# Moving the preparation of MLP 2's weight pairs to other steps of MLP 1

## The chip, the cores and the metric

The kernel runs on one core of one Trainium2 chip. The metric is device time in microseconds (us). Three runs of the kernel before took 1110.99, 1112.35 and 1111.3 us, so the median is 1111.3 us. A separate profiled execution of it took 1110.82 us, and its span from the first to the last instruction is 1109.0 us.

## The reference

Windowed attention with eight memory keys over 3072 tokens of width 512 is followed by two MLPs with a hidden width of 2048. Weights come as 64-bit floats and are rounded to 32 bits on the chip.

```python
def _moe_ref(x, w_in, w_out):       # MLP 1
    h = x @ w_in
    g = h - np.tanh(h)
    return (g @ w_out).astype(np.float32)

def _moe2_ref(x, w_in, w_out):      # MLP 2
    h = x @ w_in
    g = np.where(h >= 1, h, np.where(h <= -1, 0.0, (h + 1) ** 2 / 4))
    return (g @ w_out).astype(np.float32)

x = attention(q, k, v, mem_k, mem_v)     # chunks of 32, left 16, right 8
x = _moe_ref(x, **moe); return _moe2_ref(x, **moe2)
```

## The kernel before, in words

The engines are named as in the profile: PE multiplies matrices, DVE is the vector engine, ACT the activation engine, SP issues the transfers (DMAs). PSUM is the memory that PE writes to. Every engine works through a list of instructions in the order in which the program was written, and an instruction that waits holds up all that stand behind it on its engine.

Every operand of a product is kept as a high and a low half (`hi`, a rounded copy made on ACT; `lo`, the rest, subtracted on DVE by `split_to`, lines 224 and 225), and a product is the sum of three: hi x hi, hi x lo, lo x hi.

**MLP 1** works on six blocks of 512 tokens. Each block takes 16 steps, one for every 128 hidden columns, so there are 96 steps, 0 to 95. A step has `hidden` (12 matmuls into a PSUM tile `h`, of which there are two), and `gate` (tanh on ACT, a subtraction on DVE that frees `h` for the step after the next). On DVE each step also makes the low half of the weights two steps ahead (`split_weights_lo`, tile `wlo0`). In steps 16 to 79 a step also has `output`, the second product of the step 16 earlier (blocks 0 to 3, again 12 matmuls), whose weights SP loads again for each block (`w1o_load`, line 196). Attention for the later blocks runs between the steps up to step 78, one group of 128 tokens every four steps (`slot_v`, `slot_s`, `slot_exp`, `slot_b`).

The second product of the last two blocks is made after step 95 with fewer multiplications, from sums of quarters (Strassen and Winograd): seven passes of eight products, `G(-1, 0)` to `G(-1, 55)`, each of six matmuls (`last_product`, line 815). The quarters of MLP 1's second weights that these need are the "own" sums: `own_raw`, `prep_sums` and `own_split`, placed by `OWN_AT`. The sums of the gated values are `g_sums` (lines 683 to 686), and each pass product needs a split of its values on ACT and DVE (`prepare`, tiles `ghi` and `glo`, five of each).

**MLP 2** does both its products in that way, on three stretches of 1024 tokens (`sb` = 0, 1, 2): products `P(sb, q, i)` with q = 0 to 7 and i from 1 to 7 (`product`, line 727), then passes `G(sb, k)`. After a product 1 or 6, ACT copies the PSUM tile out (`take_copy`, line 651, tiles `u1`, `u2`), after a 5 the same into `v`; only then may PE go on in that tile, with product 6, 7 or 3. Products 2, 7, 3 and 4 each end in a gate (`gate2`: an addition on DVE, line 661, two ACT instructions, lines 665 and 666, and one on DVE, line 669).

MLP 2's weights are prepared in 16 **pairs** (`PAIRS`; eight of the first weights, eight of the second). Preparing one pair takes
- `prep_load`: two DMAs of 512 KB;
- `prep_act`: four ACT instructions (lines 136 and 139);
- `prep_rest`, twice: four DVE instructions each (lines 145, 146, 154, 159);
- `prep_sums`: four DVE instructions on half tiles (line 220);
- `prep_split`, four parts: a high half on ACT (224), a low half on DVE (225);
- `prep_store`: seven DMAs of 256 KB.

The dictionaries `before`, `rounds` and `behind` say what is written at which step: `before` and `rounds` ahead of `hidden` and `gate` of the next step, `behind` after them. `late` holds what is written among the products that follow the steps; its second part counts only products 1, 4, 2 and 7 of sb = 0 ("events").

```python
        run(before, i)
        run(rounds, i)
        hidden(i + 1, EARLY_N if i + 1 < 2 else 0)
        gate(i + 1)
        run(behind, i)
        if 0 <= o < PLAIN:
            output(o)
```

Eleven pairs begin in MLP 1 at steps 33, 37, 41, ..., 77 (every 4.4 steps); two are prepared among the passes G(-1), at k = 6 to 38; the last three among the products of sb = 0, one item at every event.

Of the kernel before, what the change touches and what calls it, by code (L numbers as in the profile page):

```python
# [30 lines left out]
KC = DM // 128  # L31
FC = DFF // 128
# [24 lines left out]
HALF = FC // 2  # L57
NSB = NB // 2
PAIRS = [(w, q) for w in range(2) for q in range(HALF)]
PREP, PREP_EVERY, PREP_FIRST, PREP_LATE = 33, 4.4, 11, 2  # L60
STREAM = 10
W1O, GSETS = 4, 5
EXTRA = 0

PLAIN = (NB - 2) * FC
OWN_AT = {q: 2 * FC + (0 if q % 2 == 0 else FC) + 2 * q for q in range(HALF)}

SPACE_A = (3, 4)

# [7 lines left out]
def tile_memory_attention_two_mlps(  # L77
# [463 lines left out]
    spare = []  # L541
# [62 lines left out]
    NG2 = len(PASSES) * HALF  # L604
# [193 lines left out]
    def last_product(e):  # L798
        _, sb, k = e
        i, q = PASSES[k // HALF], k % HALF  # L800
        a = i in (1, 6, 7, 4)
        if q == 0 and i in (1, 2, 5):
            bank[a] = [ps_g[0].tile([128, 512], F32, tag=f"g{c}{1 - a}", name=f"acc{i}_{sb}_{c}") for c in range(2)]
        rests()
        prepare(sb, k)
        hi_g, lo_g = gsplit.pop((sb, k))
        tag, t = w_t.pop(e)
        hi, lo = t[:, :256], t[:, 256:]
        first, last = i in (1, 2, 5) and q == 0, q == HALF - 1
        products = [(j, c) for j in range(3) for c in range(2)]  # L810
        if last:
            products.sort(key=lambda p: p[1])
        for j, c in products:
            w, g = ((hi, hi_g), (lo, hi_g), (hi, lo_g))[j]
            nc.tensor.matmul(  # L815
                bank[a][c], w[:, c * 128:(c + 1) * 128], g,
                start=first and j == 0, stop=last and j == 2, skip_group_check=True,
            )
        load_w(tag)
        flush()  # L820
        if k in SUMS_AT[sb < 0]:
            g_sums(sb, *SUMS_AT[sb < 0][k])
        for j in range(1, GSETS):
            prepare(sb, k + j)
        if last:
            done(sb, i, bank[a])
        nxt = sb + 1
        if nxt < NSB:
            for f, *args in x_at[sb < 0].get(k, ()):
                f(nxt, *args)  # L830

    x_at = [
        {2: [(x_load,)], 8: [(x_sum, 5)], 10: [(x_sum, 6)], 12: [(x_sum, 7)], 14: [(x_sum, 3)]},
        {18: [(x_load,)], 22: [(x_sum, 5)], 24: [(x_sum, 6)], 26: [(x_sum, 7)], 28: [(x_sum, 3)]},
    ]
    for n, i in enumerate((1, 2, 6, 5, 7, 3, 4)):
        for k in range(2):
# [33 lines left out]
            else:  # L871
                nc.sync.dma_start(out=out[(dm + c) * 128:(dm + c + 1) * 128, b * N:(b + 1) * N], in_=y[c])

    late = [{}, {}]
    for n, p in enumerate(PAIRS[PREP_FIRST:]):
        f = [
            (prep_act, *p), (prep_rest, *p, 0), (prep_rest, *p, 1), (prep_sums, *p),
            (prep_split, *p, 0), (prep_split, *p, 1), (prep_split, *p, 2), (prep_split, *p, 3),
        ]
        f = [[x] for x in f] + [[] for _ in range(1)]  # L880
        for m in range(4):
            f[5 + m].insert(0, (prep_store, *p, m))
        if n + PREP_FIRST + 1 < len(PAIRS):
            f[3].append((prep_load, *PAIRS[n + PREP_FIRST + 1]))
        for k, x in enumerate(f):
            if n < PREP_LATE:
                late[0].setdefault(6 + 2 * (8 * n + k), []).extend(x)
            else:
                late[1].setdefault(8 * (n - PREP_LATE) + k, []).extend(x)

    before, rounds, behind = {}, {}, {}

    def at_step(events, i, f, *args):
        assert i >= 0
        events.setdefault(int(i), []).append((i, f, args))


    for t in range(PER, NG + 1):
        k = t - PER
        i = SPACE_A[0] * min(k, PER) + SPACE_A[1] * max(0, k - PER)  # L900
# [12 lines left out]
    for w in range(2):  # L913
        for fc in range(FC):
            p = fc - EARLY + w * (FC + 2)
            assert p < fc + w * LAG - 2 + w
            if p >= 0:
# [3 lines left out]
                at_step(rounds, p, round_rest, 0, w, fc)  # L921
    for q, o in OWN_AT.items():
        at_step(rounds, o, own_raw, q, o - FC)
# [3 lines left out]
        at_step(before, o + 2, prep_store, 2, q, 1)  # L927
        at_step(before, o + 3, prep_store, 2, q, 2)
    for n, pair in enumerate(PAIRS):
        p = int(PREP + PREP_EVERY * n)  # L930
        if n > PREP_FIRST:
            break
        at_step(behind, p - 3, prep_load, *pair)
        if n == PREP_FIRST:
            break
        at_step(before, p, prep_act, *pair)
        at_step(rounds, p, prep_rest, *pair, 0)
        at_step(rounds, p + 1, prep_rest, *pair, 1)
        at_step(behind, p + 1, prep_sums, *pair)
        for m in range(4):  # L940
            at_step((rounds, behind)[m % 2], p + 2 + m // 2, prep_split, *pair, m)
            at_step(before, p + 3 + m // 2 + 0.1 * m, prep_store, *pair, m)
# [4 lines left out]
    LAST = NS - FC  # L947
# [3 lines left out]
    for i in range(STREAM):  # L951
        at_step(before, LAST + 1 + i // 2, stream_in)
    for q in range(HALF // 2):
        at_step(behind, LAST + 2 * q + 1, g_sums, -1, q, 0)
        at_step(behind, LAST + 2 * q + 2, g_sums, -1, q, 1)
    for k in range(3):
        at_step(behind, NS - 4 + k, prepare, -1, k, True)
        if k < 2:
# [11 lines left out]
    for j in range(PER):  # L970
        w = 0, 0, j
        pool, tag = ((ps_a, "a"), (ps_acc, "acc0"))[j % 2]
        pair = pool.tile([128, 2, 512], F32, tag=tag, name=f"start_a{j}")
# [80 lines left out]
    events = 0  # L1054
    for e in plan:
        if e[0] == "P":
            product(e)
        else:
            last_product(e)
        f = []  # L1060
        if e[0] == "G" and e[1] < 0:
            f = late[0].pop(e[2], [])
            if e[2] == NG2 - 1:
                spare.extend(f"y{i}" for i in range(KC))
        elif e[0] == "P" and e[1] == 0 and e[3] in (1, 4, 2, 7):
            f = late[1].pop(events, [])
            events += 1
            if not late[1] and f:
                spare.extend(f"prep{i}" for i in range(9))
        for f, *args in f:  # L1070
            f(*args)
    assert not late[0] and not late[1]
    assert not before and not rounds and not behind


# [46 lines left out]
```

## Time and profile before

| | |
|---|---|
| median of three runs | 1111.3 us |
| profiled execution, its span | 1110.82 us, 1109.0 us |
| PE busy | 1068.8 us (96%) |
| DVE busy | 858.0 us (77%) |
| ACT busy | 641.3 us (58%) |
| PE, DVE in the passes G(-1, 15) to G(-1, 33), 39.3 us | 31.6 us, 34.8 us |
| PE, DVE, ACT among products of sb = 0, 73.3 us | 59.0 us, 53.7 us, 48.5 us |

Busy time is the time in which at least one instruction runs on the engine. Matmuls overlap: the record of one is longer than the distance to the next, so a product's length is read from the starts. DVE instructions overlap slightly in the same way.

### The profile page before, as it was taken

What the parts mean: (1) busy time and instruction counts of PE and PEld (TensorE: products, weight loads), DVE (VectorE), ACT (ScalarE), POOL (GpSimd) and SP (SyncE); (2) the same over time, 40 slices, a digit from 0 to 9 for tenths busy, and PEclk for the clock granted to TensorE, in tenths of its full rate; (3) what the DMA queues carried; (4) which work ended last, traced back from release to release, by engine and by line L of the source; (5) the groups of instructions that cost most, each with busy time, mean ns of one, the idle gap of its engine ahead of it and who ended that gap; (6) DMA issues with size and microseconds to landing.
All of it is one profiled execution on the core that took longest, in us unless ns stands there. A gap on an engine that the chain in (4) does not pass through costs nothing.

```text
span 1109.0 us, 21044 instructions
## 1 busy us (share of the span) xinstructions
PE 1068.8 (96%) x7607; PEld 862.5 (78%) x7607; DVE 858.0 (77%) x1520; ACT 641.3 (58%) x1128; POOL 42.6 (4%) x38
## 2 busy tenths in 40 slices
PE   7899999999999999999989978899999999999998
PEld 3677888888888888888857855687888888888887
DVE  4799977799898987767889677688567697467854
ACT  3566665555555554544656566766467766477553
POOL 1132221000000000000000000000000000000000
PEclk8999999999999999999999999999999999999999
DMA  9997885899898999634479876786776787766674
GB/s 221 255 249 202 261 243 178 257 299 315 283 308 269 290 276 329 219 118 139 125 270 319 267 234 226 223 262 210 231 214 193 208 273 212 234 192 194 197 207 150
DMA packets 211944, 259.36 MB, mean 234 GB/s; under 512 B 65409, under 2 KB 128897, under 8 KB 211841
## 3 DMA queue, kind: packets, MB, share of 16 engines
q1 hardware_dynamic: 211840, 258.01, 76.2%
q8 instruction: 61, 1.00, 0.4%
q14 instruction: 43, 0.34, 0.1%
HBM read 199.23 MB, written 58.72 MB: 233 GB/s over the span
## 4 chain that ended last, share of the span: by engine, by line
PE 87%; DVE 5%; ACT 4%; DMA 2%; issue 1%; SPq 0%; DVEq 0%; ACTq 0%
PE h L488 24%; PE acc L815 20%; PE acc L526 16%; PE qa L727 9%; PE qc L727 4%; PE qb L727 2%; PE acc_-1_0_6986 L815 2%; PE acc_-1_1_6987 L815 2%; PE a L392 1%; PE a L336 1%; ACT t L665 1%; ACT t L666 1%; PE b L378 1%; DVE g L661 1%; PE start_tx L963 1%
## 5 line engine op out<-in xcount | busy, mean ns | idle before, releaser
L815 PE MATMUL acc<-ghi,inG 128*128 128x512 f32 x672 | 183.1, 389 | 0.0
L501 ACT ACTIVATE g<-h 128x512 f32<-128x512 f32 x96 | 57.4, 598 | 196.2 <-PE h L488 159.6
L727 PE MATMUL qa<-xc,inP 128*128 128x512 f32 x576 | 145.6, 399 | 13.8 <-ACT u L651 11.8
L815 PEld LDWEIGHTS acc<-ghi,inG 128*128 128x128 f32 x672 | 126.1, 188 | 26.2
L225 DVE TENSOR_TENSOR glo<-g,ghi 128x512 fp32r<-128x512 f32 x174 | 118.0, 687 | 31.7 <-ACT ghi L224 30.9
L727 PEld LDWEIGHTS qa<-xc,inP 128*128 128x128 f32 x576 | 109.1, 191 | 42.6 <-ACT u L651 15.6
L224 ACT ACTIVATE ghi<-g 128x512 fp32r<-128x512 f32 x174 | 107.5, 627 | 46.5 <-PE acc L815 23.0
L815 PE MATMUL acc<-glo,inG 128*128 128x512 f32 x336 | 107.2, 390 | 0.4 <-DVE glo L225 0.3
L502 DVE TENSOR_TENSOR g<-h,g 128x512 f32<-128x512 f32 x96 | 66.1, 688 | 53.4 <-ACT g L501 52.1
L488 PE MATMUL h<-xh,whi 128*128 128x512 f32 (+2 forms) x392 | 105.4, 391 | 0.0
L488 PE MATMUL h<-xl,whi 128*128 128x512 f32 (+2 forms) x392 | 104.0, 387 | 0.1
L488 PE MATMUL h<-xh,wlo 128*128 128x512 f32 (+2 forms) x392 | 103.7, 386 | 0.0
L665 ACT ACTIVATE t<-g,half 128x512 f32<-128x512 f32 x72 | 52.2, 724 | 74.5 <-DVE g L661 74.5
L488 PEld LDWEIGHTS h<-xl,whi 128*128 128x128 f32 x392 | 73.0, 188 | 15.4 <-DVE xl L423 0.2
L488 PEld LDWEIGHTS h<-xh,wlo 128*128 128x128 f32 x392 | 73.0, 188 | 14.8
L178 DVE TENSOR_TENSOR wlo<-raw,whi 128x512 fp32r<-128x512 f32 x112 | 79.6, 711 | 5.1 <-ACT whi L171 5.1
L488 PEld LDWEIGHTS h<-xh,whi 128*128 128x128 f32 x392 | 71.8, 188 | 15.0 <-ACT xh L418 0.3
L171 ACT ACTIVATE whi<-raw 128x512 fp32r<-128x512 f32 x112 | 70.1, 626 | 8.0 <-POOL raw L159 8.0
L815 PEld LDWEIGHTS acc<-glo,inG 128*128 128x128 f32 x336 | 62.9, 188 | 14.7 <-DVE glo L225 1.9
L727 PE MATMUL qc<-xc,inP 128*128 128x512 f32 x288 | 73.5, 391 | 0.5 <-ACT v L651 0.5
L526 PE MATMUL acc<-ghi,whi 128*128 128x512 f32 x256 | 74.0, 403 | 0.0
L526 PE MATMUL acc<-ghi,wlo 128*128 128x512 f32 x256 | 70.7, 390 | 0.0
(713 smaller groups left out, 1802.5 us busy)
## 6 DMA issues: line engine op xcount, KB each, us to landing
inP<-part SPq DMA_DIRECT2D x168, 256.0 KB, 3.0
inG<-part SPq DMA_DIRECT2D x168, 256.0 KB, 2.9
stage<-w_in SPq DMA_DIRECT2D x32, 512.0 KB, 5.5
stage<-w_out SPq DMA_DIRECT2D x32, 512.0 KB, 4.7
part<-preph SPq DMA_DIRECT2D x64, 256.0 KB, 4.3
whi<-w1o SPq DMA_DIRECT2D x48, 256.0 KB, 4.9
wlo<-w1o SPq DMA_DIRECT2D x48, 256.0 KB, 5.0
part<-prepl SPq DMA_DIRECT2D x48, 256.0 KB, 4.5
```

Source lines behind the costliest of these rows:

```text
L171: nc.scalar.activation(out=hi, in_=r, func=AF.Copy)
L178: nc.vector.tensor_tensor(out=lo, in0=r, in1=hi.bitcast(F32), op=ALU.subtract)
L224: nc.scalar.activation(out=hi, in_=src, func=AF.Copy)
L225: nc.vector.tensor_tensor(out=lo, in0=src, in1=hi.bitcast(F32), op=ALU.subtract)
L336: nc.tensor.matmul(sp[j * CHUNK:(j + 1) * CHUNK, hh, pr, :], qt[j][hh * D:(hh + 1) * D, pr, :], kt[j][hh * D:(hh + 1) * D, pr, :], start=T ...
L488: nc.tensor.matmul(hp, w[:, kc * 128:(kc + 1) * 128], x[:, kc, n0:n1], start=j == 0 and kc == 0, stop=j == 2 and kc == KC - 1,)
L501: nc.scalar.activation(out=g, in_=hp, func=AF.Tanh)
L502: nc.vector.tensor_tensor(out=g, in0=hp, in1=g, op=ALU.subtract)
L526: nc.tensor.matmul(acc_t[dm], w[:, dm * 128:(dm + 1) * 128], g, start=first and j == 0, stop=last and j == 2,)
L665: nc.scalar.activation(out=t, in_=h, func=AF.Relu, scale=0.5, bias=half)
L727: nc.tensor.matmul(o, w[:, k * 128:(k + 1) * 128], z[k], start=i in (1, 2, 5) and j == 0 and k == 0, stop=j == 2 and k == 1, skip_group_ch ...
L815: nc.tensor.matmul(bank[a][c], w[:, c * 128:(c + 1) * 128], g, start=first and j == 0, stop=last and j == 2, skip_group_check=True,)
```

## The change

A pair now begins every four steps, at steps 30, 34, ..., 78, and two more at 83 and 90: fifteen pairs in MLP 1. None is prepared among the passes G(-1). The sixteenth, (1, 7), has one item at every third event, from event 2 to event 26 (the last only stores). The own sums go from steps 32, 36, 40, 44 and 50, 54, 58, 62 to 48, 52, 56, 60 and 66, 70, 74, 78 (in `OWN_AT` blocks are counted from the step; the second product of a step stands 16 steps behind it, so these are blocks 2 and 3 of the outputs). `g_sums` for q = 0 to 3 go two steps later. The load of the next stretch's input (`x_load`) goes from G(-1, 18) to G(-1, 14).

```diff
-PREP, PREP_EVERY, PREP_FIRST, PREP_LATE = 33, 4.4, 11, 2
+PREP_AT = [30 + 4 * n for n in range(13)] + [83, 90]
+PREP_FIRST = len(PREP_AT)
...
-OWN_AT = {q: 2 * FC + (0 if q % 2 == 0 else FC) + 2 * q for q in range(HALF)}
+OWN_AT = {q: 3 * FC + (0 if q % 2 == 0 else FC) + 2 * q for q in range(HALF)}
...
-        {18: [(x_load,)], 22: [(x_sum, 5)], ...
+        {14: [(x_load,)], 22: [(x_sum, 5)], ...
...
-    late = [{}, {}]
-    for n, p in enumerate(PAIRS[PREP_FIRST:]):
+    late = {}
+    for p in PAIRS[PREP_FIRST:]:
...
-            if n < PREP_LATE:
-                late[0].setdefault(6 + 2 * (8 * n + k), []).extend(x)
-            else:
-                late[1].setdefault(8 * (n - PREP_LATE) + k, []).extend(x)
+            late[2 + 3 * k] = x
...
-        at_step(behind, LAST + 2 * q + 1, g_sums, -1, q, 0)
-        at_step(behind, LAST + 2 * q + 2, g_sums, -1, q, 1)
+        at_step(behind, LAST + 2 * q + 3, g_sums, -1, q, 0)
+        at_step(behind, LAST + 2 * q + 4, g_sums, -1, q, 1)
...
-        if e[0] == "G" and e[1] < 0:
-            f = late[0].pop(e[2], [])
...
-            f = late[1].pop(events, [])
+            f = late.pop(events, [])
```

Three places show what this does to the lists. The first is DVE between the low weight halves of steps 86 and 87 (`wlo0_86`, `wlo0_87`), near the end of MLP 1; before, these were:

```order
L178 TENSOR_TENSOR wlo0_86_6734<-raw00_6_833,whi0_86_6732 128x512
L502 TENSOR_TENSOR g85_6753<-h85_6740,g85_6753 128x512
L686 TENSOR_TENSOR g82_6673<-g66_5645,g82_6673 128x512
L178 TENSOR_TENSOR wlo0_87_6759<-raw00_7_897,whi0_87_6757 128x512
L502 TENSOR_TENSOR g86_6778<-h86_6765,g86_6778 128x512
```

And now (line numbers are one higher; `raw11`, `stage11` and `sums1` belong to a pair):

```order
L179 TENSOR_TENSOR wlo0_86_6833<-raw00_6_833,whi0_86_6831 128x512
L146 TENSOR_SCALAR raw11_13_6801<-raw11_13_6801 128x512
L147 TENSOR_SCALAR raw11_13_6801<-raw11_13_6801 128x512
L155 SCALAR_TENSOR_TENSOR raw11_13_6801<-stage11_13_6728,raw11_13_6801 128x512
L160 ISA raw11_13_6801<-stage11_13_6728,raw11_13_6801 128x1024
L503 TENSOR_TENSOR g85_6856<-h85_6843,g85_6856 128x512
L221 TENSOR_TENSOR sums1_5_6859<-raw11_5_6798 128x256
L221 TENSOR_TENSOR sums1_5_6859<-raw11_13_6801,raw11_5_6798 128x256
L221 TENSOR_TENSOR sums1_5_6859<-raw11_13_6801,sums1_5_6859 128x256 x2
L687 TENSOR_TENSOR g80_6658<-g64_5422,g80_6658 128x512
L179 TENSOR_TENSOR wlo0_87_6867<-raw00_7_897,whi0_87_6865 128x512
```

A second `prep_rest` stands ahead of the gate of step 85, and `prep_sums` between that gate and the weights of step 87.

The second place is DVE in the passes, from the low half for G(-1, 26) on (`glo2`; `s5`, `s6`, `a7`, `a4` and `xc1` are the input sums of the next stretch). Before:

```order
L225 TENSOR_TENSOR glo2_-1_26_7367<-s1_-1_2_6781,ghi2_-1_26_7366 128x512
L590 TENSOR_TENSOR s5_0_0_7370<-a7_0_0_7298,a4_0_0_7300 128x512
L590 TENSOR_TENSOR s5_0_1_7371<-a7_0_1_7299,a4_0_1_7301 128x512
L225 TENSOR_TENSOR glo2_-1_27_7390<-s1_-1_3_6826,ghi2_-1_27_7389 128x512
L225 TENSOR_TENSOR glo2_-1_28_7408<-s1_-1_4_7013,ghi2_-1_28_7407 128x512
L590 TENSOR_TENSOR s6_0_0_7411<-s5_0_0_7370,xc1_0_7296 128x512
L590 TENSOR_TENSOR s6_0_1_7412<-s5_0_1_7371,xc1_0_7296 128x512
L145 TENSOR_SCALAR raw11_4_7375<-raw11_4_7375 128x512
L146 TENSOR_SCALAR raw11_4_7375<-raw11_4_7375 128x512
L154 SCALAR_TENSOR_TENSOR raw11_4_7375<-stage11_4_7195,raw11_4_7375 128x512
L159 ISA raw11_4_7375<-stage11_4_7195,raw11_4_7375 128x1024
L225 TENSOR_TENSOR glo2_-1_29_7428<-s1_-1_5_7054,ghi2_-1_29_7427 128x512
```

Now:

```order
L226 TENSOR_TENSOR glo2_-1_26_7509<-s1_-1_2_6962,ghi2_-1_26_7508 128x512
L591 TENSOR_TENSOR s5_0_0_7512<-a7_0_0_7392,a4_0_0_7394 128x512
L591 TENSOR_TENSOR s5_0_1_7513<-a7_0_1_7393,a4_0_1_7395 128x512
L226 TENSOR_TENSOR glo2_-1_27_7525<-s1_-1_3_7007,ghi2_-1_27_7524 128x512
L226 TENSOR_TENSOR glo2_-1_28_7543<-s1_-1_4_7201,ghi2_-1_28_7542 128x512
L591 TENSOR_TENSOR s6_0_0_7546<-s5_0_0_7512,xc1_0_7390 128x512
L591 TENSOR_TENSOR s6_0_1_7547<-s5_0_1_7513,xc1_0_7390 128x512
L226 TENSOR_TENSOR glo2_-1_29_7559<-s1_-1_5_7242,ghi2_-1_29_7558 128x512
```

The four instructions of `prep_rest` are gone from between the low halves; the input sums stay where they were.

The third place is ACT among the products of sb = 0, from the gate of product P(0, 1, 4) on (`t2_0_1_21`) to the copy of product 6 of q = 2 (`u2_0_2`). Before:

```order
L665 ACTIVATE t2_0_1_21_8111<-qa0_1_7953,half_83 128x512
L666 ACTIVATE t2_0_1_21_8111<-t2_0_1_21_8111 128x512
L136 ACTIVATE raw11_6_8115<-stage11_6_7969 128x512
L139 ACTIVATE stage11_6_7969<-stage11_6_7969 128x512
L136 ACTIVATE raw11_14_8118<-stage11_14_7971 128x512
L139 ACTIVATE stage11_14_7971<-stage11_14_7971 128x512
L651 ACTIVATE u2_0_2_8129<-qa0_2_8071 128x512
L665 ACTIVATE t2_0_2_11_8143<-g2_0_2_11_8141,half_83 128x512
```

Now:

```order
L666 ACTIVATE t2_0_1_21_8169<-qa0_1_8039,half_83 128x512
L667 ACTIVATE t2_0_1_21_8169<-t2_0_1_21_8169 128x512
L652 ACTIVATE u2_0_2_8184<-qa0_2_8134 128x512
L666 ACTIVATE t2_0_2_11_8198<-g2_0_2_11_8196,half_83 128x512
L667 ACTIVATE t2_0_2_11_8198<-t2_0_2_11_8198 128x512
```

The four instructions of `prep_act` no longer stand ahead of that copy; the remaining pair's four stand ahead of `u1_0_1`, at event 2.

## Rows read from the trace of the kernel before

**Rows 1.** The page: span, and busy time of the engines

```profile
span 1109.0 us, 21044 instructions
PE 1068.8 (96%) x7607; PEld 862.5 (78%) x7607; DVE 858.0 (77%) x1520; ACT 641.3 (58%) x1128; POOL 42.6 (4%) x38
```

**Rows 2.** Busy time by stretch: start:end, length, engines, granted clock, DMA

```profile
core 0: us, PE busy (x) PEld busy (x) DVE busy (x) ACT busy (x) POOL busy (x), PEclk, DMA share, GB/s
201.00:298.20 97.20, 97.20 (x929) 80.33 (x929) 88.23 (x170) 52.73 (x98) 0.00 (x0) 1.00 0.93 290
397.70:491.70 94.00, 94.00 (x852) 77.46 (x851) 71.61 (x138) 45.27 (x88) 0.00 (x0) 1.00 0.72 231
491.70:534.40 42.70, 42.70 (x190) 35.34 (x189) 30.52 (x48) 19.20 (x35) 0.00 (x0) 1.00 0.39 129
554.80:594.10 39.30, 31.62 (x116) 22.85 (x115) 34.82 (x64) 21.29 (x40) 0.00 (x0) 0.91 0.84 291
579.10:582.40 3.30, 3.30 (x9) 2.66 (x9) 3.21 (x6) 1.49 (x3) 0.00 (x0) 0.55 1.08 397
594.10:637.60 43.50, 43.50 (x194) 36.01 (x193) 34.01 (x60) 25.00 (x44) 0.00 (x0) 1.00 0.88 279
637.60:710.90 73.30, 59.00 (x224) 42.57 (x223) 53.66 (x95) 48.45 (x87) 0.00 (x0) 0.95 0.73 235
```

**Rows 3.** Waits of PE from 534 to 720 us: total, times, longest

```profile
PE qa L727 <- ACT u L651: 11.8, 9, 2.8
PE acc_-1_0_7397 L815 <- DVE glo_-1_27_7390 L225: 2.7, 1, 2.7
```

**Rows 4.** Timeline of DVE, passes: start, length, instruction, [idle before, releaser]

```profile
577.07 0.69 DVE L590 TENSOR_TENSOR s<-a,a 128x512 f32<-128x512 f32 x1 [4.20 <-DMA a<-yd]
...
585.43 0.42 DVE L145 TENSOR_SCALAR raw<-raw 128x512 f32<-128x512 f32 x1
...
587.68 0.68 DVE L225 TENSOR_TENSOR glo_-1_31_7460<-s_-1_7_7152,ghi_-1_31_7459 128x512 fp32r<-128x512 f32 x1
```

**Rows 5.** Timeline of DVE, passes: sums and splits of a pair

```profile
557.68 0.41 DVE L220 TENSOR_TENSOR sums<-raw 128x256 f32<-128x256 f32 x1
...
559.14 0.68 DVE L225 TENSOR_TENSOR glo_-1_17_7208<-s_-1_1_6729,ghi_-1_17_7207 128x512 fp32r<-128x512 f32 x1
...
561.55 0.75 DVE L225 TENSOR_TENSOR prepl<-raw,preph 128x256 fp32r<-128x256 f32 x2
562.23 0.68 DVE L225 TENSOR_TENSOR glo_-1_19_7240<-s_-1_3_6827,ghi_-1_19_7239 128x512 fp32r<-128x512 f32 x1
562.83 0.68 DVE L785 TENSOR_TENSOR g<-g,s_-1_3_6827 128x512 f32<-128x512 f32 x1
```

**Rows 6.** Timeline of ACT among the products of sb = 0

```profile
653.23 0.65 ACT L136 ACTIVATE raw<-stage 128x512 f32<-128x512 f32 x1
...
655.49 0.57 ACT L651 ACTIVATE u<-qa 128x512 f32<-128x512 f32 x1
```

**Rows 7.** Timeline of DVE at the gate of step 84

```profile
505.31 0.69 DVE L502 TENSOR_TENSOR g<-h,g 128x512 f32<-128x512 f32 x1 [0.83 <-ACT g L501]
505.92 0.68 DVE L683 TENSOR_TENSOR s_-1_1_6728<-g,g 128x512 f32<-128x512 f32 x1
```

**Rows 8.** Timeline of PE, hidden product of step 86

```profile
507.20 1.07 PE L488 MATMUL h<-xh,whi 128*128 128x512 f32 x4
...
509.01 1.07 PE L488 MATMUL h<-xh,wlo 128*128 128x512 f32 x4
```

**Rows 9.** Timeline of ACT among undisturbed products, sb = 1, q = 5

```profile
857.26 0.58 ACT L651 ACTIVATE u<-qa 128x512 f32<-128x512 f32 x1
```

**Rows 10.** Timeline of PE there: products 4 and 6, six matmuls each

```profile
857.69 2.88 PE L727 MATMUL qa<-xc,inP 128*128 128x512 f32 x12
```

**Rows 11.** Timeline of DVE there

```profile
857.89 0.69 DVE L661 TENSOR_TENSOR g<-qc,u 128x512 f32<-128x512 f32 x1 [0.76 <-PE qc L727]
...
861.97 0.69 DVE L661 TENSOR_TENSOR g<-qb,u 128x512 f32<-128x512 f32 x1 [1.24 <-PE qb L727]
```

**Rows 12.** Timeline of SP at step 65 and 68: loads of output weights

```profile
401.63 0.42 SPq L196 DMA_DIRECT2D whi<-w1o  x1
...
416.29 0.38 SPq L196 DMA_DIRECT2D whi<-w1o  x1
```

More of the change, by code (lines that the diff above doesn't have):

```diff
@@ L833, in tile_memory_attention_two_mlps @@
         {2: [(x_load,)], 8: [(x_sum, 5)], 10: [(x_sum, 6)], 12: [(x_sum, 7)], 14: [(x_sum, 3)]},
-        {18: [(x_load,)], 22: [(x_sum, 5)], 24: [(x_sum, 6)], 26: [(x_sum, 7)], 28: [(x_sum, 3)]},
+        {14: [(x_load,)], 22: [(x_sum, 5)], 24: [(x_sum, 6)], 26: [(x_sum, 7)], 28: [(x_sum, 3)]},
     ]
@@ L879, in tile_memory_attention_two_mlps @@
         ]
-        f = [[x] for x in f] + [[] for _ in range(1)]
+        f = [[x] for x in f] + [[]]
         for m in range(4):
             f[5 + m].insert(0, (prep_store, *p, m))
-        if n + PREP_FIRST + 1 < len(PAIRS):
-            f[3].append((prep_load, *PAIRS[n + PREP_FIRST + 1]))
         for k, x in enumerate(f):
-            if n < PREP_LATE:
-                late[0].setdefault(6 + 2 * (8 * n + k), []).extend(x)
-            else:
-                late[1].setdefault(8 * (n - PREP_LATE) + k, []).extend(x)
+            late[2 + 3 * k] = x
     before, rounds, behind = {}, {}, {}
@@ L929, in tile_memory_attention_two_mlps @@
     for n, pair in enumerate(PAIRS):
-        p = int(PREP + PREP_EVERY * n)
-        if n > PREP_FIRST:
+        if n == PREP_FIRST:
+            at_step(behind, PREP_AT[-1] + 2, prep_load, *pair)
             break
+        p = PREP_AT[n]
         at_step(behind, p - 3, prep_load, *pair)
-        if n == PREP_FIRST:
-            break
         at_step(before, p, prep_act, *pair)
@@ L1059, in tile_memory_attention_two_mlps @@
             last_product(e)
-        f = []
-        if e[0] == "G" and e[1] < 0:
-            f = late[0].pop(e[2], [])
-            if e[2] == NG2 - 1:
-                spare.extend(f"y{i}" for i in range(KC))
-        elif e[0] == "P" and e[1] == 0 and e[3] in (1, 4, 2, 7):
-            f = late[1].pop(events, [])
+        if e[0] == "G" and e[1:] == (-1, NG2 - 1):
+            spare.extend(f"y{i}" for i in range(KC))
+        if e[0] == "P" and e[1] == 0 and e[3] in (1, 4, 2, 7):
+            f = late.pop(events, [])
             events += 1
-            if not late[1] and f:
+            for x, *args in f:
+                x(*args)
+            if f and not late:
                 spare.extend(f"prep{i}" for i in range(9))
-        for f, *args in f:
-            f(*args)
-    assert not late[0] and not late[1]
+    assert not late
     assert not before and not rounds and not behind
```

## The prediction

> **What bounds the kernel now.** I read the busy table first. PE is busy for 1068.8 of 1109.0 us [rows 1], so the time is PE's, and a change of order can only win what PE loses by waiting. Next I read busy time by stretch, to see where it loses. In steps 32 to 47 PE is busy for 97.20 of 97.20 us although DVE works 88.23 us (91%); steps 65 to 80 and the steps after them are full as well [rows 2]. From 594.1 to 637.6 us, 43.5 us hold 32 undisturbed products of six matmuls, so one takes 1.36 us [rows 2]. That unit turns two other stretches into losses. From 554.8 to 594.1 us stand the 19 passes G(-1, 15) to G(-1, 33): 19 x 1.36 = 25.9 us of work in 39.3 us, so 13.4 us are lost. From 637.6 to 710.9 us stand 37 products of sb = 0: 50.4 us of work in 73.3 us, 22.9 us lost. Together 36.3 us, the most that this change can win there.
>
> Then I asked who was waited for. Among the products PE waits 11.8 us for ACT's copies `u`, nine times; among the passes its longest wait is 2.7 us for DVE's low half of G(-1, 27) [rows 3]. The timelines show what stands ahead of these. Four instructions of `prep_act` run from 653.23 us to the copy at 655.49: 2.26 us that PE's next product spends waiting [rows 6]. A `prep_rest` runs from 585.43 to 587.68 us, 2.25 us, directly ahead of the low half of G(-1, 31) [rows 4]. DVE works 34.8 of 39.3 us there against 34.0 of 43.5 in the stretch after [rows 2]. One wait has another root: DVE stood still for 4.20 us for a transfer of the input sums, ahead of the 2.7 us wait [rows 4]. The clock adds to it: after that wait the granted clock is 0.55 for 3.3 us, near the lower level of 1.2 GHz, and means over the two stretches are 0.91 and 0.95 [rows 2]; those losses are within the 36.3 us.
>
> **What a pair costs DVE.** By starts that follow each other directly: `prep_rest` 2.25 us [rows 4]; `prep_sums` 559.14 - 557.68 = 1.46 us; two half splits 0.68 us and a full instruction 562.83 - 562.23 = 0.60 us [rows 5], so the splits of a pair of the second weights (two halves, two full, one half) take 2.2 us. Sum: 2 x 2.25 + 1.46 + 2.2 = 8.2 us.
>
> **Passes.** Two pairs leave, 16.4 us of DVE; of it the second pair's `prep_rest` and `prep_sums` and the first's sums and splits, some 10 us, stood in the stretch that loses. DVE's need there falls from 34.8 to about 25 us, against 25.9 us of PE. The load of the input is issued four passes, 5.4 us, earlier, more than the 4.20 us that DVE stood still, and SP no longer meets pair stores behind a late DVE. What is late next is DVE's list itself, one low half (0.60 us) and one sum (0.60 us) per product in passes 16 to 23, just under 1.36 us; five `glo` tiles let it run up to four products ahead, and that is its cover. I take the whole 13.4 us as won; the bounds are 13.4 and, if the transfer still arrives late, 13.4 minus the 4.4 us lost at passes 27 and 28 with the low clock.
>
> **Products of sb = 0.** Three dense pairs cost 22.9 us, 7.6 each. One pair stays, an item every third event. In undisturbed products the copy `u` ends at 857.84 us and product 6 starts 1.36 us behind 857.69, at 859.05 [rows 9, 10]: 1.2 us of slack. DVE stands still for 0.76 and 1.24 us per q [rows 11]. `prep_act` stands behind product 7, ahead of `u1`: 2.26 - 1.2 = 1.1 us lost. The first `prep_rest` stands behind product 2, ahead of the addition of product 7, whose gate precedes the same copy: 2.25 - 1.2 = 1.0 us. The second stands behind product 4 and meets the two idle times, 2.0 us, so 0.2. `prep_sums` meets 0.76 us, the rest is within the slack: 0. Of the four splits the one behind product 2 makes DVE wait for ACT and then work ahead of the same addition: 0.7 us; the others 0. Sum 3.0 us; bounds 0 (spread thin enough to hide) and 7.6 us (as dear as a dense pair).
>
> **Steps 30 to 79.** Thirteen pairs begin every four steps, where before eleven began every 4.4. In steps 65 to 80 DVE worked 71.6 of 94.0 us [rows 2]. Four own sums come in, each two additions, `prep_sums` and two splits: 4 x 0.60 + 1.46 = 3.9 us, and about half a pair: 71.6 + 15.4 + 4.1 = 91 us, 97%. That is above the 91% that the trace shows with PE undisturbed. What covers it: behind a hidden product stand three products of twelve matmuls before its `h` tile is written again, 36 x 0.227 = 8.2 us (0.91 us for four) [rows 8], of which a gate needs some 1.5 (one product less the slack of 1.2 in the next part). A step that begins a pair and an own sum has 7.3 us of DVE work in 5.4 us, the next 6.7, and the two after them 5.0 and 3.7, so DVE falls 3 us behind and catches up: within 6 us of cover. Cost 0; if the cover fails, up to 5 us.
>
> **Steps 81 to 95.** Here no output stands between hidden products, and cover is thin. A step is 12 matmuls, 2.72 us [rows 8]. The gate of step 84 runs from 505.31 to 506.00 us, and the product that needs its tile starts at 507.20 [rows 7, 8]: 1.2 us of slack. Per step DVE has a gate (505.92 - 505.31 = 0.61 us) and a low weight half (0.60), and the sums of a q add 1.32 us in one step and 0.60 in the next. With the pair that begins at 83, steps 83 to 86 hold 4.8 + 3.8 + 8.2 = 16.8 us of DVE in 10.9 us. I followed the list by these lengths from the end of the hidden product of 83. The gate of 84 is still in time; behind it stand the sums, `wlo0_86` and the second `prep_rest`, so the gate of 85 ends at 9.6 where product 87 was due at 8.0: 1.7 us lost. `wlo0_87` then comes 1.0 us late behind `prep_sums`, `wlo0_88` 0.9 us, the gates between 0.2: 3.8 us, after which DVE has caught up by step 89. The pair at 90 meets only one sum: 0.9 at the gate of 91, 1.3 at that of 92, 0.4 at `wlo0_94`, 0.1: 2.8 us. ACT's `prep_act` delays a tanh by 0.6 us, inside these. Sum 6.6 us. Bounds: 0, and all of both pairs, 16.4 us; I take 6.6, since the gate rows give both the need and the slack.
>
> **Sum.** -13.4 - 22.9 + 3.0 + 6.6 = -26.7 us on the profiled execution's 1110.8 us: 1084.1. It stands 0.5 us below the median of the runs, so 1084.6 us there.
>
> **A rule to weigh.** In rows 5 DVE instructions start 0.60 us apart although each is recorded with 0.68 us. [...]
>
> **Rivals.**
> 1. The late steps hide the pairs. DVE is idle there for 12.2 of 42.7 us [rows 2], and ACT's slack or the earlier load might let the pairs slip in. For: 30.5 us of DVE in 42.7. Against: the idle time lies between gates, 0.83 us at a time [rows 7]. Then -36.3 + 3.0: 1078 us.
> 2. The late steps cost all of their pairs: a low half or a load of the pair comes late on top, and a wait over 2 us brings the lower clock as at 579.1 us [rows 2]. For: that clock followed waits of 2.7 us. Against: my longest wait there is 1.7 us. -36.3 + 3.0 + 16.4: 1094 us.
> 3. The passes keep losing, since the input transfer and not the pairs held them. For: the 4.20 us [rows 4]. Against: most other waits stand behind pair items. If half of 13.4 stays: 1091 us.
> 4. DVE is the bound in steps 65 to 80. If an instruction there needs its record's 0.68 us and not 0.60, the 91 us become 103 in 94: 1084.6 + 9 = 1094 us. For: 91 us is more than any stretch shows. Against: starts 0.60 us apart [rows 5].
> 5. Slower: SP becomes the bound in steps 48 to 79, where own stores, pair stores, attention and the loads of output weights now meet in both blocks. From 401.63 to 416.29 us SP issued 19 transfers without a pause, 0.77 us each [rows 12], and the lists hold 25 to 34 transfers per four steps (24.3 us), where 30 need 23.1. It decides from 0.92 us per transfer on: 30 of them then take 27.7 us, 3.4 more than the steps, eight times over, which eats the gain; at 1.0 us it is 5.7 x 8 = 46 us, and the time 1130 us. Against: the densest four steps had 34 before, too, and PE lost nothing.
> 6. The change does nothing: the losses come from the products' own chain. Against: sb = 1 runs the same products without a wait [rows 10, 11]. 1111 us.
>
> **Numbers.** The forecast 0.64; rival 1 0.10; 2 0.09; 3 0.06; 4 0.05; 5 0.04; 6 0.02. This measurement can tell about 0.2% (2 us) from no change. Faster by more than that are the forecast and rivals 1 to 4: 0.94; same 0.02; slower 0.04. The forecast's own range comes from its bounds, 3.0 between 0 and 7.6 and 6.6 between 3 and 11: 1078 to 1093. Rival 1 lies at its lower end and 2 and 4 at its upper; 1077 to 1094 leaves out less than 2 in 10.
>
> **What would show it.** Right: PE full in passes 15 to 33, one or two short waits for `u` early in sb = 0, and waits of PE on the gate or `wlo0` in steps 85 to 88 and 91 to 94, 4 to 10 us in all; DVE over 93% in steps 64 to 79 with PE full. Wrong: PE waiting between steps 48 and 79, for loads (`whi<-w1o`) or for DVE; a lower granted clock near step 87; waits for the input transfer in passes 26 to 28.

## The result, and the profile after

Four runs of the changed kernel took 1085.57 to 1086.88 us, median 1086.55, beside 1110.99 to 1112.35 us of the kernel before on the same chip: ratio 0.9774, 95% interval 0.9757 to 0.9791. The forecast was 1084.6 us (1077 to 1094). The profiled execution took 1086.51 us, its span is 1084.7.

The page of the changed kernel answers to [rows 1]:

```profile
span 1084.7 us, 21054 instructions
PE 1058.1 (98%) x7601; PEld 858.2 (79%) x7607; DVE 857.1 (79%) x1520; ACT 642.3 (59%) x1128; POOL 42.5 (4%) x38
```

DVE and ACT do the same work. Of the 24.3 us by which the span is shorter, 13.6 are idle time of PE (40.2 before, 26.6 now) and 10.7 are busy time. Before, the granted clock was 0.91 and 0.95 on average in the two stretches that lost, so part of the loss there was slow matmuls and not waiting: at most some 7 us (0.09 x 39.3 + 0.05 x 73.3, an estimate from [rows 2]); the rest is not split up here. Busy time by stretch answers to [rows 2], in the same order: steps 32 to 47, steps 65 to 80, steps 81 to 95, passes 15 to 33, and the 37 products of sb = 0 that took 73.3 us before (224 matmul records in both windows):

```profile
core 0: us, PE busy (x) PEld busy (x) DVE busy (x) ACT busy (x) POOL busy (x), PEclk, DMA share, GB/s
199.90:297.10 97.20, 97.20 (x930) 80.32 (x929) 76.94 (x147) 50.35 (x94) 0.00 (x0) 1.00 0.87 271
397.10:491.10 94.00, 94.00 (x852) 77.47 (x851) 85.99 (x170) 53.30 (x103) 0.00 (x0) 1.00 0.80 266
491.10:542.40 51.30, 45.45 (x190) 34.39 (x189) 47.43 (x88) 28.75 (x56) 0.00 (x0) 1.00 0.74 248
562.90:588.70 25.80, 25.80 (x116) 21.36 (x115) 23.52 (x40) 16.01 (x28) 0.00 (x0) 1.00 0.89 294
633.40:686.50 53.10, 51.99 (x224) 41.20 (x223) 42.78 (x72) 37.55 (x65) 0.00 (x0) 1.00 0.73 215
```

The passes are full: 25.8 us where there were 39.3. The products need 53.1 us instead of 73.3. The steps 81 to 95 need 51.3 us instead of 42.7, with DVE at 47.43 us of them; that is what the change gives back. The granted clock is 1.00 in all five stretches; before it was 0.91 and 0.95 in two.

The waits of PE from 481 to 542 us, and, in the second fence, from 542 to 720 us (what answers to [rows 3]); the columns are total, times and longest:

```profile
PE h L489 <- DVE g L503: 3.9, 4, 1.8
PE h L489 <- DVE wlo L179: 0.8, 2, 0.5
PE h L489 <- ACT whi L172: 0.8, 1, 0.8
```

```profile
PE qa L728 <- ACT u L652: 1.9, 4, 0.9
```

Comparing, in the two traces, the end of every hidden product and the start of every product, the difference of 24.3 us between the spans is: start of the kernel -1.2, steps 12 to 80 +0.6, steps 81 to 95 +8.65, passes -13.4, products of sb = 0 -22.9 + 3.85; what remains, 0.1, is rounding. The 1.2 us at the start go with the granted clock there, 0.96 on average over the first 40 us against 0.91 before; the program is the same there.

### The profile page after: what moved, and what is told of

Its sections match the earlier page's. It is cut to its first block, busy times and chain, and to the rows that moved or that the text cites. A ratio compares the mean times of both kernels' runs of the same rounds, so it can differ in the third digit from the quotient of the medians.

```text
span 1084.7 us, 21054 instructions
## 1 busy us (share of the span) xinstructions
PE 1058.1 (98%) x7601; PEld 858.2 (79%) x7607; DVE 857.1 (79%) x1520; ACT 642.3 (59%) x1128; POOL 42.5 (4%) x38
## 4 chain that ended last, share of the span: by engine, by line
PE 83%; DVE 6%; ACT 4%; DMA 4%; SPq 2%; issue 1%; DVEq 0%; ACTq 0%
PE h L489 20%; PE acc L816 18%; PE acc L527 16%; PE qa L728 10%; PE qc L728 5%; PE qb L728 3%; PE acc_-1_1_7175 L816 2%; PE acc_-1_0_7174 L816 2%; PE a L393 1%; PE a L337 1%; ACT t L666 1%; PE acc_-1_1_7533 L816 1%; PE acc_-1_0_7532 L816 1%; PE b L379 1%; ACT t L667 1%
## 5 line engine op out<-in xcount | busy, mean ns | idle before, releaser
L728 PE MATMUL qa<-xc,inP 128*128 128x512 f32 x576 | 140.8, 391 | 2.0 <-ACT u L652 1.9
```

The source lines that it names most:

```text
L728: nc.tensor.matmul(o, w[:, k * 128:(k + 1) * 128], z[k], start=i in (1, 2, 5) and j == 0 and k == 0, stop=j == 2 and k == 1, skip_group_ch ...
```

## The experiments

They ran on other executions and other chips (the kernel before: medians of 1109.96, 1110.23 and 1111.0 us beside them), so ratios are compared, and where a loss lies is read from the traces: lateness of a product against its undisturbed length (1.36 us for six matmuls), or the step in which a hidden product falls behind the same one of the changed kernel.

**The input's load back at pass 18.**

```diff
-        {14: [(x_load,)], 22: [(x_sum, 5)], ...
+        {18: [(x_load,)], 22: [(x_sum, 5)], ...
```

> The changed kernel, with the load of the first input halves (x_load) back behind pass G(-1, 18) instead of 14; everything else as changed. Theory (the pairs held the passes): DVE now has 8 us to spare in passes 15 to 33, so at most the still stand of 4.2 us ahead of pass 27 returns: 0 to +4.4 us, 1086.5 to 1091, best guess 1088, all of it in passes 24 to 30. Rival (the late transfer held the passes): half or all of the 13.4 us come back, 1093 to 1100 us.

1085.55 us, ratio 0.9784 (0.9768 to 0.9800). No pass loses anything. DVE does stand still for the transfer, nearly as long as in [rows 4] (timeline of DVE in this run):

```profile
571.39 0.69 DVE L226 TENSOR_TENSOR glo_-1_26_7509<-s_-1_2_6962,ghi_-1_26_7508 128x512 fp32r<-128x512 f32 x1 [0.60 <-ACT ghi_-1_26_7508 L225]
576.10 1.35 DVE L591 TENSOR_TENSOR s<-a,a 128x512 f32<-128x512 f32 x2 [4.02 <-DMA a<-yd]
```

The same 4 us cost PE 2.7 us before and nothing now: without pair items DVE has worked its `glo` tiles ahead when the transfer holds it. Here it ended the low half of pass 26 at 572.08 us, 4.3 us before that pass began; before, 1.1 us ahead. The rival is refuted, and the best guess of 1088 us was too high: the earlier load is worth nothing that the times or the trace show.

**The own sums back in the earlier steps,** that is 32 to 44 and 50 to 62 instead of 48 to 60 and 66 to 78.

```diff
-OWN_AT = {q: 3 * FC + ...
+OWN_AT = {q: 2 * FC + ...
```

> The changed kernel, with the sums of MLP 1's own weights (OWN_AT) back in blocks 2 and 3 counted as before (steps 32 to 47) instead of 48 to 63. Theory (a busy DVE costs nothing as long as its backlog stays under some 6 us): DVE at about 94% in steps 32 to 47 and lower in 48 to 63, no loss in either, 1086.5 us give or take 1. Rival (the move was needed, steps 32 to 47 overflow with pairs every four steps): PE waits for gates or wlo there, 2 us or more, 1089 to 1092.

1084.86 us, ratio 0.9776 (0.9762 to 0.9791): no difference that the times show. The trace shows where it differs: nothing is lost in steps 32 to 47, where DVE is now busy for 94% (91.6 of 97.3 us), the hidden product of step 62 gains 0.2 and that of step 82 gains 1.03 us. There the changed kernel waits for `whi`, the third line of its first fence of waits above. Its DVE, at the end of block 3 (timeline):

```profile
492.17 0.68 DVE L226 TENSOR_TENSOR sums<-sums,ownh 128x512 fp32r<-128x512 f32 x1
492.76 0.42 DVE L221 TENSOR_TENSOR sums<-raw 128x256 f32<-128x256 f32 x1
...
494.23 1.28 DVE L538 COPY y<-acc 128x512 f32<-128x512 f32 x2
```

and its ACT:

```profile
494.95 1.20 ACT L536 ACTIVATE y<-acc 128x512 f32<-128x512 f32 x2 [3.35 <-DVE y L538]
496.04 0.62 ACT L172 ACTIVATE whi<-raw 128x512 fp32r<-128x512 f32 x1
```

ACT's own copies of the block's result were held 3.35 us by DVE's copies of it, which stood behind an own split and the sums of pair 12; `whi` stood behind ACT's. With the own split gone the wait is gone.

**Three pairs among the products again.**

```diff
-PREP_AT = [30 + 4 * n for n in range(13)] + [83, 90]
+PREP_AT = [30 + 4 * n for n in range(13)]
...
-            late[2 + 3 * k] = x
+            late.setdefault(8 * n + k, []).extend(x)
```

> The changed kernel with only the 13 pairs every four steps; the pairs at steps 83 and 90 go back among MLP 2's first products, three pairs there, one item behind every event, as before the change. Theory (pair items cost what they delay): steps 85 to 95 lose nothing more, -7.5 us (the wait for whi at step 82 stays, 1.1), the products of sb = 0 lose 22.9 instead of 3.9, +19: 1098 us. Rival (the products lost because the passes ahead of them ran late and left ACT or the weight loads behind): with undisturbed passes they lose under half of it, 1086 us or less.

1098.53 us, ratio 0.9894 (0.9879 to 0.9909), as the theory has it. Steps 82 to 95 lose nothing (-7.5 us against the changed kernel), the products of sb = 0 lose 24.1 us although the passes ahead of them ran without loss, and the waits are of the kind of [rows 3] again:

```profile
PE qa L728 <- ACT u L652: 13.4, 9, 2.8
PE qa L728 <- DVE g L662: 1.0, 2, 0.5
PE qc L728 <- ACT v L652: 0.3, 2, 0.2
```

**The pair of step 90 among the passes.**

```diff
-PREP_AT = [...] + [83, 90]
+PREP_AT = [...] + [83]
...
+            (late if n else late_g)[2 + 3 * k if n else 36 + 2 * k] = x    # late_g: behind pass k
...
```

> The changed kernel with the pair at step 90 moved among passes G(-1, 36) to G(-1, 52), one item behind every second pass; the pair at 83 and the last pair stay. Theory (a pair costs nothing where DVE has its 8 us idle in small pieces and glo tiles run ahead): the 3.2 us of steps 93 to 95 go, the passes lose 0 to 3: 1083.3 to 1086.5, best guess 1084. Rival (any item of 2.2 us ahead of a glo stops PE in the passes, as in passes 15 to 33 of the kernel before, at some 7 us a pair): 1089 to 1091 us.

1085.57 us, ratio 0.9781 (0.9766 to 0.9795). The 3.2 us of steps 93 to 95 went, and passes 45 and 47 lost some 1.7: a gain of some 1.4 in the trace, too little for the times. Here a `prep_rest` and a `prep_sums` stand ahead of the low halves that PE needs next:

```profile
PE acc_-1_0_7485 L816 <- DVE glo_-1_47_7794 L226: 0.7, 1, 0.7
PE acc_-1_0_7485 L816 <- DVE glo_-1_45_7755 L226: 0.4, 1, 0.4
```

**Only the pairs moved.** The three edits that move no pair are undone together:

```diff
+OWN_AT = {q: 2 * FC + ...
...
+        {18: [(x_load,)], ...
...
+        at_step(behind, LAST + 2 * q + 1, g_sums, -1, q, 0)
+        at_step(behind, LAST + 2 * q + 2, g_sums, -1, q, 1)
```

> The changed kernel with only its pairs moved: the load of the first inputs (x_load) back behind pass 18, the own sums (OWN_AT) back in steps 32 to 47, MLP 1's group sums (g_sums) back two steps earlier. Theory (all the gain is the pairs'): passes 15 to 33 still lose nothing, the wait for whi at step 82 is gone as in the run own_back, and the sums still stand on the pair at 83: 1085 us give or take 1.5. Rival (the passes' 13.4 us were won by the three small moves together, which only hide one another when undone singly): 1090 to 1099 us, the loss in passes 15 to 33.

1084.0 us, ratio 0.9764 (0.9747 to 0.9782). The passes lose nothing, so the moved pairs alone win them. With the sums two steps earlier the pair at 90 loses 1.2 us instead of 3.2. The one at 83 loses 4.9 instead of 4.35; part of this is a stretch of 3.4 us that was granted half the clock.

**Group sums four steps later,** on the version with a pair among the passes:

```diff
-        at_step(behind, LAST + 2 * q + 3, g_sums, -1, q, 0)
-        at_step(behind, LAST + 2 * q + 4, g_sums, -1, q, 1)
+        at_step(behind, LAST + 2 * q + 7, g_sums, -1, q, 0)
+        at_step(behind, LAST + 2 * q + 8, g_sums, -1, q, 1)
```

> The run pass14 (pair at 83, one pair among the passes, one among the products) with MLP 1's group sums four steps later (steps 87 to 94 instead of 83 to 90). Theory (the pair at 83 loses because it meets these sums: 13.0 instead of 16.8 us of DVE in four steps of 10.9): the 4.35 us of steps 86 to 89 fall to about 1, the sums fit into the idle time of steps 87 to 95: 1082.3 us. Rival (the pair's own lumps of 2.2 us stand ahead of the gates, sums or not): 1085.5 us, with the same waits at steps 86 to 89.

1083.66 us, ratio 0.9762 (0.9742 to 0.9781). The trace shows the expected place and nearly the size: steps 83 to 90 lose 1.4 us instead of 4.35. The times alone do not separate it from the run that it builds on (0.9781, 0.9766 to 0.9795). PE's waits from 480 to 536 us:

```profile
PE h L489 <- ACT whi L172: 0.8, 1, 0.8
PE h L489 <- DVE g L503: 0.6, 2, 0.5
```

**Smaller pieces in steps 83 to 95,** on the changed kernel:

```diff
-        at_step(rounds, p, prep_rest, *pair, 0)
-        at_step(rounds, p + 1, prep_rest, *pair, 1)
-        at_step(behind, p + 1, prep_sums, *pair)
+        if n > 12:                                               # the last two pairs of the steps
+            for i in range(2):
+                at_step(before, p + i, one_act, *pair, i, None)  # half of prep_act
+                at_step(rounds, p + i, one_mag, *pair, i)        # two instructions of prep_rest
+                at_step(behind, p + i, one_sign, *pair, i)       # the other two
+            at_step(behind, p + 2, prep_sums, *pair)
+            p += 1
+        else:                                                    # as before
...
```

> The changed kernel with the pairs at 83 and 90 in smaller pieces over one step more: each prep_act in two, each prep_rest as 0.7 us ahead of the gate and 1.2 us behind it, prep_sums and splits a step later, stores after the splits. Theory: the pair at 90 (no sums beside it after step 90) fits, its 3.2 us fall to 1 or less, while the pair at 83 stays on the group sums, 16.8 us of DVE work in four steps of 10.9, and still loses 3 to 4.4: 1083 to 1084.5 us. Rival A (only the lumps ahead of the gates cost): both go, 1079.5 us. Rival B (only the amount of DVE work counts): 1086.5 us.

1084.26 us, ratio 0.9765 (0.9749 to 0.9781). The pair at 83 still loses 4.0 us, the one at 90 0.95 instead of 3.17, but 0.8 are lost in passes 1, 2, 25 and 26. In the trace both rivals fail: pieces free most of the pair that has room and do next to nothing for the one that stands on the sums. The times alone rule out rival A; the changed kernel's 0.9774, which is rival B, lies within this interval.

**Smaller pieces among the products,** on the changed kernel:

```diff
-            late[2 + 3 * k] = x
+        late = {
+            0: [(one_act, *p, 0, 0)], 1: [(one_act, *p, 0, 1)], 2: [(one_act, *p, 1, 0)],
+            3: [(one_act, *p, 1, 1), (one_mag, *p, 0)], 4: [(one_sign, *p, 0)],
+            7: [(one_mag, *p, 1)], 8: [(one_sign, *p, 1)], 11: [(prep_sums2, *p, 0)], 12: [(prep_sums2, *p, 1)],
+            15: [(prep_split, *p, 0)], 16: [(prep_store, *p, 0), (prep_split, *p, 1)],
+            19: [(prep_store, *p, 1), (prep_split, *p, 2)], 20: [(prep_store, *p, 2), (prep_split, *p, 3)],
+            23: [(prep_store, *p, 3)],
+        }
...
```

> The changed kernel with the last pair in smaller items among MLP 2's first products: prep_act in four pieces behind four events, prep_rest in four (0.7 or 1.2 us each), prep_sums in two, each behind an event of its own. Theory (an item costs what it exceeds the 1.2 us of slack by): the products of sb = 0 lose 0 to 0.8 instead of 3.85 us: 1083 to 1084 us. Rival (each item costs something, since ACT and DVE hand over to each other at every product): 3.85 us or more stay lost: 1086.5 us or above.

1085.64 us, ratio 0.9782 (0.9761 to 0.9802); in the trace the products lose 2.4 us instead of 3.85. The expected 0 to 0.8 was missed, and the times show no gain over the changed kernel (0.9774). All pieces up to event 15 cost nothing, but the splits behind events 16 and 20 cost 0.9 and 1.5. The timeline of ACT, then of DVE, at event 16:

```profile
659.70 0.63 ACT L684 ACTIVATE t<-t 128x512 f32<-128x512 f32 x1
660.23 0.61 ACT L242 ACTIVATE preph<-sums 128x512 fp32r<-128x512 f32 x1
```

```profile
660.88 0.69 DVE L243 TENSOR_TENSOR prepl<-sums,preph 128x512 fp32r<-128x512 f32 x1 [2.62 <-ACT preph L242]
661.49 0.69 DVE L687 SCALAR_TENSOR_TENSOR g<-t,g 128x512 f32<-128x512 f32 x1
662.09 0.69 DVE L679 TENSOR_TENSOR g<-qb,u 128x512 f32<-128x512 f32 x1
```

My price for an item had left out its order: ACT makes the high half only behind a gate's two instructions, and DVE, whose list has the low half next, stands still 2.62 us ahead of two instructions that PE's chain needs. The length of that standstill is not the price by itself. In the changed kernel the split behind event 20 makes DVE stand still for 2.62 us too, and PE loses only 0.15; there PE had just lost 0.8 us to the split behind event 17 and needed DVE later, which is argued from the timelines and not tested.

**All that the theory asks for, together.** Own sums back in the earlier steps, group sums in 87 to 94, pair 13 (counted from 0) from step 82 in pieces, pair 14 in pieces behind passes 28 to 53, the last pair as in the run above.

> All that the theory asks for: own sums in steps 32 to 47 (-1.3), group sums four steps later, the fourteenth pair begun at step 82 with each prep_rest in two pieces, the fifteenth among passes G(-1, 28) to G(-1, 53) in pieces of at most 1.2 us, the last one thin among the products. Theory: steps 81 to 95 lose under 1 us instead of 8.65, the passes under 1, the products under 1 instead of 3.85: 1075 to 1078 us. Rival (losses move elsewhere: the pieces delay glo halves that stood in time, or DVE is full from step 81 to pass 53, idle 21 us against 16.4 of pairs): 1081 us or more.

1076.54 us, ratio 0.9705 (0.9681 to 0.9729). Steps 81 to 95 lose 0.2 us, the passes nothing, the products 2.4 at the same two splits. Then these four splits went behind events 15, 19, 23 and 27:

> The run best1 with the four splits of the last pair each behind a first product of a quarter (P(0,q,1), events 15, 19, 23, 27) instead of two of them behind P(0,q,4), where ACT reached its half of the split only after a gate that waits for DVE and DVE stood 2.4 to 2.6 us at the other half. Theory (an item that hands over from ACT to DVE costs what it makes DVE stand in order behind ACT): the 2.4 us that the products of sb = 0 still lose go, 1074 us, 0.2% under best1. Rival (the loss moves with the splits): 1076.5 us.

1075.09 us, ratio 0.9673 (0.9657 to 0.9689): the best version, 3.3% under the kernel before. Between the two the ratios' intervals overlap; the traces show the products' loss fall from 2.4 to 0.4 us. The splits moved behind another product and also farther apart (every fourth event instead of two in a row), so which of the two counts is not separated. The end of step 78 to step 95 of the best version, its passes, and the products of sb = 0:

```profile
482.00:536.00 54.00, 54.00 (x241) 44.41 (x240) 46.57 (x85) 29.30 (x56) 0.00 (x0) 1.00 0.54 180
536.00:609.30 73.30, 73.30 (x325) 60.67 (x325) 71.62 (x122) 47.80 (x84) 0.00 (x0) 1.00 0.80 259
609.30:685.90 76.60, 76.48 (x338) 62.94 (x337) 54.00 (x88) 55.49 (x94) 0.00 (x0) 1.00 0.79 240
```

PE is full with DVE at 71.62 of 73.3 us (98%) in the passes: here, how much DVE has to do in a stretch does not tell what it costs, as long as it is below the stretch's length and in pieces that fit.

## Why the prediction was right, point by point

**Passes, -13.4.** Measured -13.4. The reason held: the pairs, and not the transfer, made the loss (the runs with x_load at 18 and with only the pairs moved). The remark on the earlier load, "more than the 4.20 us that DVE stood still", was beside the point.

**Products, -22.9 and +3.0.** Measured -22.9 and +3.85. `prep_act` was put at 1.1 and lost 1.2 with the slow matmul after the wait. ACT's timeline at event 2, and PE's, answer to [rows 6]:

```profile
627.70 0.64 ACT L137 ACTIVATE raw<-stage 128x512 f32<-128x512 f32 x1
...
629.91 0.58 ACT L652 ACTIVATE u<-qa 128x512 f32<-128x512 f32 x1
```

```profile
628.13 1.52 PE L728 MATMUL qa<-xc,inP 128*128 128x512 f32 x6
630.54 1.20 PE L728 MATMUL qa<-xc,inP 128*128 128x512 f32 x4 [0.89 <-ACT u L652]
```

The first `prep_rest` (1.0 expected) lost 0.95, the second (0.2) nothing, the split at event 17 (0.7 expected) 0.8. The splits at events 20 and 23 were costed at 0 and lost 0.15 and 0.8. At event 23 the cause is one that the sum lacked: from q = 6 on ACT also makes `ghi` copies for the passes, and one stands ahead of this split's; DVE, with the low half next in its list, stood still ahead of product 3's addition:

```profile
679.81 0.62 ACT L775 ACTIVATE ghi<-g 128x512 fp32r<-128x512 f32 x1
680.33 0.41 ACT L225 ACTIVATE preph<-raw 128x256 fp32r<-128x256 f32 x1
```

```profile
680.76 0.43 DVE L226 TENSOR_TENSOR preph<-raw,preph 128x256 fp32r<-128x256 f32 x1 [1.57 <-ACT preph L225]
681.11 0.69 DVE L662 TENSOR_TENSOR g<-qc,u 128x512 f32<-128x512 f32 x1
```

This is the mechanism that the run with smaller pieces met again at events 16 and 20.

**Steps 30 to 79, 0.** Measured 0.6, at steps 50 and 62; the profile does not say what ended the wait at step 62. The prediction named PE waiting there as a sign of being wrong: it came, but small. The largest lag of a gate behind its hidden product in steps 48 to 79 was 3.6 us, at step 51, and the cover of 6 us held with DVE at 85.99 of 94 us in steps 65 to 80 (91%, not the 97% that I added up: the last own split, the sums of pair 12 and its splits, some 4 us, fell behind the stretch, at 492 us in the rows above). In steps 64 to 79 it was 91% as well, so the sign "DVE over 93%" did not come. The fullest steps were 48 to 63, which the working did not look at: DVE was busy for 91.91 of 97.8 us (94%), and the 0.6 us were lost there.

**Steps 81 to 95, +6.6.** Measured 8.65; this is the term whose size was most off. The pair at 83 lost 4.35 (3.8 expected) and that at 90 3.17 (2.8), at the instructions foreseen: gates of 85, 91 and 92, and `wlo0`. The longest wait, at the gate of 85, on PE and on DVE:

```profile
509.63 1.11 PE L489 MATMUL h<-xh,wlo 128*128 128x512 f32 x4
512.49 0.70 PE L489 MATMUL h<-xh,whi 128*128 128x512 f32 x2 [1.76 <-DVE g L503]
```

```profile
509.40 0.42 DVE L146 TENSOR_SCALAR raw<-raw 128x512 f32<-128x512 f32 x1
...
511.05 0.69 DVE L160 CUSTOM_DVE_ANT_0 raw<-stage,raw 128x1024 uint16<-128x1024 uint16 x1
511.66 0.68 DVE L503 TENSOR_TENSOR g<-h,g 128x512 f32<-128x512 f32 x1
```

The gate of 85 stands behind the second `prep_rest`, as in the working; 1.7 us were expected, the profile shows a wait of 1.76, and by the starts product 87 was held 1.9 us (the wait counts from the end of the last record, which lies beyond the next possible start). What the sum lacked is the wait for `whi` at step 82, 1.13 us, which comes from the own sums moved to block 3 and was costed at 0 (own_back), and about 0.1 us of slow first matmuls behind each wait. The range took 3 to 11 us for this term, where the working had given 0 and 16.4 as bounds; neither 3 nor 11 is worked out there.

**The rivals.** The late steps neither hid the pairs (1) nor cost all 16.4 us of them, and no low clock came in this execution (2). That is partly luck: rival 2 asked for a wait over 2 us against the expected 1.7, but with only the pairs moved 1.75 us at the same place were followed by half the clock (last section). The transfer did not hold the passes (3). DVE did not bind in steps 65 to 80 (4): there its instructions start 0.60 us apart with records of 0.68 to 0.69, and 85.99 us busy left PE full. The Trainium skill (VectorE: DVE Perf Modes, "The DRAIN you can't avoid") has the next instruction wait until the pipeline is empty, but lets one that it does not count as held start earlier; the starts 0.60 us apart under records of 0.68 to 0.69 agree with the second. SP bound nothing (5): PE waited for no load of weights.

The median came out 2.0 us above the forecast, the profiled execution 2.4 above its own sum (1086.51 against 1084.1): +2.1 in steps 81 to 95, +0.85 in the products, +0.6 in the middle steps, less 1.2 at the start, which no step of the argument spoke of. That last part is luck.

## What to carry to other kernels

Price a moved piece of work by what stands behind it: its lump over the slack of the next waiter where the engine has room, and most of the overflow where the stretch holds more work than time (4.35 us lost of 16.8 - 10.9 = 5.9 with the group sums, 1.4 of 13.0 - 10.9 = 2.1 without them); the busy share alone tells neither. Where work moves into a thin stretch, look first at what else could leave it: moving the group sums saved 2.9 us that cutting the pair into pieces did not. A piece that hands over between two engines is priced in the order of both lists: the second engine stands still until the first has reached its half, and all that stands behind in its list comes later.

## What the runs showed of the hardware that was not expected

The same wait did not always bring the lower clock. At the first matmul of the hidden product of step 87 PE waited 1.76 us in the changed kernel (fence above) and 1.75 us with only the pairs moved. The stretch behind it, first of the changed kernel, then of that run:

```profile
512.60:515.80 3.20, 2.71 (x11) 1.92 (x12) 3.17 (x9) 1.75 (x4) 0.00 (x0) 1.00 1.03 351
```

```profile
512.60:515.80 3.20, 3.20 (x9) 2.49 (x8) 3.17 (x8) 1.67 (x3) 0.00 (x0) 0.50 0.59 190
```

The granted clock was 1.0 (2.4 GHz) in the one and 0.5 (1.2 GHz) in the other, with matmuls 0.43 instead of 0.23 us apart. In the runs x18 and thin_late the wait there was 1.75 and 1.76 us, and the clock stayed at 1.0. What tells them apart stays open.

Executions differ from each other at the start. From 20 to 35 us the best version's profiled run was granted 0.77 on average and the run best1 1.00, with the same instructions in that stretch of the program; by step 12 the first was 2.6 us later. That is more than the 2.0 us by which its products are better, so between the two the traces say more than the times.

At the full clock the first matmul behind a wait took 0.31 to 0.34 us to the next one instead of 0.227, some 0.1 us a wait.
